# A hand-written instruction order for linear attention, Fourier mixing and a feed-forward block on one core

## The chip, the core and the metric

The kernel runs on one core of one Trainium2 chip. The metric is the device time of one execution in microseconds (us): the time of the core from start to end, median of the runs of a kernel. The program gives each of five engines its own list of instructions, and the traces show them side by side: PE (TensorE, matmuls; PEld is its weight load), DVE (VectorE), ACT (ScalarE), POOL (GpSimd) and SP (SyncE, which here only issues DMA). The program puts PE's results in PSUM tiles, from pools with two, one and three slots (`bufs` below), and its other tiles in SBUF. The profile shows the clock granted to PE as PEclk, where 1.00 is full speed and 0.50 is half.

## The reference, cut to what matters

```python
def phi(x):                                    # 64 -> 256 features
    proj = einsum('bhsd,df->bhsf', x, w_phi)
    proj = proj - max(abs(proj), axis=-1)
    return concatenate([exp(proj), exp(-proj)])
q_p, k_p = phi(q), phi(k)                      # batch 8, heads 8, tokens 576, head size 64
kv  = einsum('bhsf,bhsd->bhfd', k_p, v);  z = sum(k_p, axis=2)
x   = (q_p @ kv) / (q_p @ z + 1e-6)            # then heads side by side: 8 x 576 x 512

u   = x + real(fft(fft(x, axis=1), axis=2))    # Fourier mixing
un  = (u - mean(u)) / sqrt(var(u) + 1e-6)
out = u + maximum(un @ w_ch1, 0) @ w_ch2       # 512 -> 2048 -> 512
```

Everything is independent from batch to batch. One batch is four kinds of work: **features** (projections of keys and queries, their maxima, the exponentials), **heads** (kv and the quotient), **mixing** (the two Fourier transforms as matmuls with cosine and sine tables, then mean and variance), and the feed-forward block, **W1** and **W2**.

## The kernel before: the parts that matter

The order of the instructions is left to an automatic scheduler. The program text runs through a batch and tells the scheduler only that the end of W1 and W2 comes first:

```python
pj = tile_pool(name="pj", bufs=2, space=PSUM)   # projections, and pn_ of the heads
pk = tile_pool(name="pk", bufs=1, space=PSUM)   # kv
pb = tile_pool(name="pb", bufs=3, space=PSUM)   # psf (W1), pso (W2), pm, psD, px, pu (mixing)
...
for b in range(B):
    X = attention(b, loaded)              # features and heads
    if b + 1 < B:
        loaded = load(b + 1)
    mixed = mixing(b, X)
    if done is not None:
        ffn(b - 1, *done)                 # W1 and W2 of the batch before
    done = mixed
ffn(B - 1, *done)
```

A head is 10 matmuls into `kv`, a copy to `kvh` (ACT), 10 matmuls into `pn_`, then `tg`, `cb`, `rd` on DVE and the head's 64 columns of `X` on POOL. Mixing uses a symmetry: columns j and 512-j of X are added and subtracted ("folded") before the transforms.

```python
# mixing, before
pm = pb.tile([128, C]); matmul(pm, ones_f, X[0:1, 0, :])   # row 0 of X on all partitions
XC = X - pm                                                # DVE, ACT for the last half block
for sl in (slice(0, 2), slice(2, 4), slice(4, 5)):         # six folds
    for dst, op in ((CE, ALU.add), (CO, ALU.subtract)):
        nc.gpsimd.tensor_tensor(out=dst[:, sl, :], in0=XC[:, sl, 0:256],
                                in1=XC[:, sl, C:256:-1], op=op)
...                                                        # four small corner fixes on POOL
# psD, px, pu: the transforms on PE, casts on ACT, additions to X on DVE
def norm(c):
    ...                                                    # bn_stats, bn_aggr on DVE
    nc.gpsimd.tensor_scalar(out=UN[...], in0=X[...], scalar1=mean, op0=ALU.subtract)
    nc.sync.dma_start_transpose(out=UT[...], in_=UN[...])  # UT feeds W1
```

(These pieces are shortened; the whole text may follow.)

The softmax here doesn't subtract the row's maximum and nothing guards it: scores larger than these inputs give would overflow.

## Time and profile before

| | before |
|---|---|
| time, median of 2 runs | 818.63 us (817.53 to 819.73) |
| span of the profiled run | 812.1 us |
| mean granted clock of PE | 0.777 |
| one steady batch | 92.3 us |
| of it, W1 and W2 | 32.8 us |

The page of the profile, first part (busy us, share of the span, number of instructions), two rows of the span in 40 slices (PE's busy tenths, and PE's clock in tenths), and the chain of work that ended last:

```profile
span 812.1 us, 10263 instructions
PE 546.9 (67%) x3992; PEld 314.6 (39%) x3992; DVE 303.8 (37%) x612; ACT 312.1 (38%) x654; POOL 316.1 (39%) x381
...
PE   0005654669765895769765896749946797649995
...
PEclk9999995569855897559955797559955698559999
...
PE 47%; ACT 14%; DMA 12%; POOL 12%; DVE 11%; issue 2%; ACTq 0%; DVEq 0%; POOLq 0%
```

The reader should look at the rows PE and PEclk together: from the ninth slice on, seven times over, PE is denser at a clock of 8 or 9 (W1 and W2), and between these stretches half idle at a clock of 5. The chain passes through PE for less than half of the span. No engine is full, and the time is a sum of stages in which one engine after another is the limit.

DVE's timeline in the heads, two heads in a row (start, duration, engine, line, operation, and in brackets the idle time ahead of it and what ended it):

```profile
328.04 0.50 DVE L394 TENSOR_TENSOR tg<-pn__2803,E 128x325 f32<-128x325 f32 x1 [1.09 <-PE pn__2803 L387]
...
330.16 0.50 DVE L394 TENSOR_TENSOR tg<-pn__2834,E 128x325 f32<-128x325 f32 x1 [0.79 <-PE pn__2834 L387]
```

One head takes 2.12 us, and DVE waits in each for PE, whose matmuls run at half clock there (0.50 from 323.00 to 338.50). PE in turn waits 0.41 us in each head for the copy `kvh` on ACT.

### The profile page before, as it was taken

What the parts mean: (1) busy time and instruction counts of PE and PEld (TensorE: products, weight loads), DVE (VectorE), ACT (ScalarE), POOL (GpSimd) and SP (SyncE); (2) the same over time, 40 slices, a digit from 0 to 9 for tenths busy, and PEclk for the clock granted to TensorE, in tenths of its full rate; (3) what the DMA queues carried; (4) which work ended last, traced back from release to release, by engine and by line L of the source; (5) the groups of instructions that cost most, each with busy time, mean ns of one, the idle gap of its engine ahead of it and who ended that gap; (6) DMA issues with size and microseconds to landing.
All of it is one profiled execution on the core that took longest, in us unless ns stands there. A gap on an engine that the chain in (4) does not pass through costs nothing.

```text
span 812.1 us, 10263 instructions
## 1 busy us (share of the span) xinstructions
PE 546.9 (67%) x3992; PEld 314.6 (39%) x3992; DVE 303.8 (37%) x612; ACT 312.1 (38%) x654; POOL 316.1 (39%) x381
## 2 busy tenths in 40 slices
PE   0005654669765895769765896749946797649995
PEld 0003322426342552426342462516433363416472
DVE  5053535534335512535335412525136332414101
ACT  3094334336044524246044443246043452316060
POOL 7045584483037701384036800385004720243000
PEclk9999995569855897559955797559955698559999
DMA  8999347143242513233152512313120011001102
GB/s 94 181 122 140 33 63 99 14 53 56 62 57 36 80 31 70 27 56 56 54 63 37 72 37 55 40 29 56 39 50 2 7 37 45 2 0 30 43 19 57
DMA packets 115681, 42.66 MB, mean 53 GB/s; under 512 B 92080, under 2 KB 110512, under 8 KB 115632
## 3 DMA queue, kind: packets, MB, share of 16 engines
q0 software_dynamic: 52288, 18.40, 20.3%
q1 hardware_dynamic: 63344, 23.61, 14.6%
q8 instruction: 31, 0.51, 0.3%
q14 instruction: 18, 0.15, 0.1%
HBM read 36.77 MB, written 9.44 MB: 57 GB/s over the span
## 4 chain that ended last, share of the span: by engine, by line
PE 47%; ACT 14%; DMA 12%; POOL 12%; DVE 11%; issue 2%; ACTq 0%; DVEq 0%; POOLq 0%
PE psf L547 16%; PE pso L560 10%; DMA out_dram<-O 8%; DMA KT<-KS 4%; ACT QPHP L367 4%; DVE MQ L324 4%; ACT QPHN L367 4%; POOL CE L426 3%; POOL CO L426 3%; PE pu L486 3%; PE kv L378 3%; PE psD L451 2%; PE pm L411 2%; DVE cb L399 1%; DVE O L566 1%
## 5 line engine op out<-in xcount | busy, mean ns | idle before, releaser
L560 PE MATMUL pso<-W2b,HT 128*128 128x512 bf16 (+1 forms) x640 | 140.4, 379 | 0.0
L547 PE MATMUL psf<-UT,W1b 128*128 128x288 bf16 x1024 | 131.5, 286 | 6.8 <-ACT HT L553 5.0
L553 ACT ACTIVATE HT<-psf 128x288 bf16<-128x288 f32 x256 | 105.2, 411 | 67.1 <-PE psf L547 50.4
L547 PEld LDWEIGHTS <-W1b 128*128 128x128 bf16 x1024 | 99.3, 98 | 37.0 <-issue 10.9
L402 POOL TENSOR_TENSOR X<-cb,rd 128x320 f32<-128x320 f32 x64 | 46.3, 724 | 152.6 <-DVE rd L401 152.3
L566 DVE SCALAR_TENSOR_TENSOR O<-pso,rs,X 128x512 f32<-128x512 f32 (+1 forms) x40 | 30.0, 749 | 196.9 <-PE pso L560 156.3
L560 PEld LDWEIGHTS <-HT 128*128 128x128 bf16 (+1 forms) x640 | 63.6, 100 | 74.1 <-issue 3.4
L473 POOL TENSOR_SCALAR UN<-X,MV 128x512 bf16<-128x512 f32 (+1 forms) x40 | 61.9, 1559 | 9.2 <-DVE MV L472 8.9
L203 POOL DMA_DIRECT2D QS<-in_q_dram x8 | 7.5, 938 | 146.6 <-DMA QT<-QS 146.6
L275 PE MATMUL psk<-wphi,KT 64*128 64x128 bf16 x256 | 19.6, 303 | 61.8 <-ACT KPn L284 32.8
L383 ACT CAST kvh<-kv 128x130 bf16<-128x130 f32 x64 | 17.8, 278 | 103.3 <-PE kv L378 103.3
L451 PE MATMUL psD<-CS,CE 128*128 128x320 bf16 x80 | 28.5, 462 | 42.5 <-POOL CE L426 28.6
L387 PEld LDWEIGHTS <-QPHN 128*128 128x128 bf16 x320 | 34.6, 127 | 54.2 <-issue 54.2
L328 ACT ACTIVATE E<-MQ 128x16 f32<-128x16 f32 x8 | 1.8, 221 | 130.3 <-DVE MQ L324 130.3
L491 DVE TENSOR_TENSOR X<-pu,X 128x511 f32<-128x511 f32 x16 | 10.8, 673 | 104.5 <-PE pu L486 104.5
L279 DVE TENSOR_REDUCE MK<-psk 128x8 f32<-128x1024 f32 x32 | 38.1, 1206 | 17.6 <-PE psk L275 17.6
L293 POOL TENSOR_TENSOR VCn<-VS,VCn 128x512 bf16<-128x512 bf16 x32 | 33.9, 1059 | 27.0 <-ACT VCn L289 25.8
L275 PEld LDWEIGHTS <-KT 64*128 64x128 bf16 x256 | 11.9, 128 | 77.2 <-issue 46.3
L284 ACT ACTIVATE KPp<-psk 128x1024 bf16<-128x1024 f32 x32 | 32.9, 1029 | 21.5 <-DVE MK L279 21.3
L387 PEld LDWEIGHTS <-QPHP 128*128 128x128 bf16 x320 | 37.8, 133 | 3.5 <-issue 3.5
L324 DVE TENSOR_REDUCE MQ<-psq 128x8 f32<-128x1024 f32 x32 | 37.4, 1207 | 0.8 <-PE psq L317 0.8
L293 POOL TENSOR_TENSOR VCp<-VS,VCp 128x512 bf16<-128x512 bf16 x32 | 33.8, 1057 | 3.8 <-ACT VCp L289 3.8
(389 smaller groups left out, 928.2 us busy)
## 6 DMA issues: line engine op xcount, KB each, us to landing
KS<-in_k_dram POOLq DMA_DIRECT2D x8, 512.0 KB, 6.0
VS<-in_v_dram POOLq DMA_DIRECT2D x8, 512.0 KB, 6.2
out_dram<-O SPq DMA_DIRECT2D x32, 128.0 KB
out_dram<-O SPq DMA_DIRECT2D x16, 256.0 KB
QS<-in_q_dram POOLq DMA_DIRECT2D x16, 128.0 KB, 3.4
QS<-in_q_dram POOLq DMA_DIRECT2D x8, 256.0 KB, 4.9
W1b<-in_moe_w_ch_dram POOLq DMA_DIRECT2D x1, 2048.0 KB, 21.2
W2b<-in_moe_w_ch_dram POOLq DMA_DIRECT2D x1, 2048.0 KB, 33.8
```

The lines of the kernel that those rows point to most:

```text
L293: nc.gpsimd.tensor_tensor(out=VC[:, hs, :, 0:D], in0=VS[:, hs, :].rearrange("p h (j d) -> p h j d", d=D), in1=VC[:, hs, :, D:D + 1].to_bro ...
L324: nc.vector.tensor_reduce(out=mv_, in_=psq[:], axis=AX.X, op=ALU.max, apply_absolute_value=True)
L367: nc.scalar.activation(out=o, in_=psh[:], func=AT.Exp, scale=sgn)
L387: nc.tensor.matmul(pn_[:, i, 65 * c:65 * c + 65], lhsT=QP[:, h, 128 * c:128 * c + 128], rhs=kvh[:, i, :], start=True, stop=True,)
L402: nc.gpsimd.tensor_tensor(out=X[:, :, D * h:D * h + D], in0=cb[:, :, 0:D], in1=rd[:].to_broadcast([128, 5, D]), op=ALU.mult,)
L426: nc.gpsimd.tensor_tensor(out=dst[:, sl, :], in0=XC[:, sl, 0:256], in1=XC[:, sl, C:256:-1], op=op)
L451: nc.tensor.matmul(ps[:], lhsT=src[:, c, 128 * mt:128 * mt + 128], rhs=mat[:, c, :], start=(c == 0), stop=(c == 4),)
L473: nc.gpsimd.tensor_scalar(out=UN[0:M, c, :], in0=X[0:M, c, :], scalar1=mv[0:M, c, 0:1], scalar2=None, op0=ALU.subtract,)
L547: nc.tensor.matmul(ps[:], lhsT=W1b[:, cc, 128 * hh:128 * hh + 128], rhs=UT[:, cc, 288 * hf:288 * hf + 288], start=(cc == 0), stop=(cc == N ...
L553: nc.scalar.activation(out=HT[:, hh, 288 * hf:288 * hf + 288], in_=ps[:], func=AT.Relu)
L560: nc.tensor.matmul(po[0:M, :], lhsT=HT[:, hh, 128 * c:128 * c + M], rhs=W2b[:, hh, :], start=(hh == 0), stop=(hh == NHH - 1),)
L566: nc.vector.scalar_tensor_tensor(out=O[0:M, :], in0=po[0:M, :], scalar=rs[0:M, c:c + 1], in1=U[0:M, c, :], op0=ALU.mult, op1=ALU.add,)
```

## The change

The intent is to give PE one dense stream at full clock. The automatic scheduler goes, and the order is written by hand. Each kind of work becomes a generator that yields where it would have to wait, with the number of pieces of W1 or W2 to put there. There are two stages per batch: A weaves heads and mixing of batch b+1 into the 32 groups of W1 of batch b; B weaves the features of batch b+2 into the 40 pairs of W2 matmuls of batch b.

```diff
-    for b in range(B):
-        X = attention(b, loaded)
-        ...
-        if done is not None:
-            ffn(b - 1, *done)
+    def weave(lead, fill=None):        # run lead; after each "yield n", n pieces of fill
+        ...
+    def mixed_from(b, made):
+        X = yield from heads(b, made)
+        if b + 1 < B:
+            fetch(b + 1)
+        return (yield from mixing(b, *X))
+    with tc.manual_schedule():
+        ...                            # loads, constants, features(0), heads(0), mixing(0), features(1)
+        for b in range(B):
+            U, UT, mv = mixed
+            rs = scales(mv)
+            wide = widen(b, UT)                                        # W1, yields per group of 4
+            if b + 1 < B:
+                mixed, HT = weave(mixed_from(b + 1, made), wide)       # stage A
+            else:
+                _, HT = weave(alone(), wide)
+            slim = narrow(b, U, rs, HT)                                # W2, yields per 2 matmuls
+            made, _ = weave(features(b + 2, *ready[b + 2]) if b + 2 < B else alone(), slim)  # B
```

The order within the heads, with the folds now made per pair of heads and before the subtraction of `pm`:

```diff
-        for h in range(H):
+        order = (4, 0, 7, 1, 6, 2, 5, 3)
+        kvh = keyvalue(order[0])
+        yield 1
+        for i, h in enumerate(order):
+            nxt = keyvalue(order[i + 1]) if i + 1 < H else None
+            combine(h, kvh)
+            if i == 0:
+                nc.gpsimd.tensor_copy(out=X[:, :, C:C + 1], in_=X[:, :, 256:257])
+            elif h in (7, 6, 5):
+                fold(7 - h)            # two POOL ops: FEO = X +- X reversed, 64 columns
+            elif h == 3:
+                fold(3)
+            kvh = nxt
+            yield 1
```

And in mixing, with the subtraction after the fold (now on DVE) and UN moved from POOL to DVE:

```diff
+        yield 7
-        matmul(pm, ones_f, X[0:1, 0, :])        -> XC (DVE, ACT), six folds and four fixes (POOL)
+        matmul(pm, ones_f, FEO[0:1, 0, :, :])
+        CEO[64:128, 4] = pm[64:128]             # ACT
+        for i in range(2):
+            CEO[:, 0:4, i] = FEO[:, 0:4, i] - pm[:, i]     # DVE
+            ...                                 # two short ops for the last half block
+        yield 5
 ...
-            nc.gpsimd.tensor_scalar(
+            nc.vector.tensor_scalar(
                 out=UN[0:M, c, :], in0=X[0:M, c, 0:C], scalar1=mv[0:M, c, 0:1], ...
```

(Both are cut to their core; the lines without code syntax are summaries.) The matmuls of the reference's arithmetic are the same: PE has 3992 of them in both kernels.

## The prediction

> **What bounds the kernel now.** I read the page first: PE is busy 67% of 812.1 us, every other engine under 40%, so no engine is full. I then cut one steady batch (275.40 to 367.70 us, 92.30 us) into its six stages by the timeline of PE and asked for a table of windows:
>
> ```profile
> core 0: us, PE busy (x) PEld busy (x) DVE busy (x) ACT busy (x) POOL busy (x), PEclk, DMA share, GB/s
> 275.40:290.60 15.20, 15.04 (x121) 11.73 (x121) 8.01 (x22) 11.99 (x31) 7.42 (x5) 1.00 0.48 74
> 290.60:308.20 17.60, 17.60 (x88) 7.98 (x87) 3.00 (x4) 0.51 (x2) 0.00 (x0) 1.00 0.17 41
> 308.20:323.00 14.80, 4.85 (x46) 2.48 (x43) 4.14 (x4) 9.04 (x13) 2.40 (x4) 0.69 0.39 77
> 323.00:338.50 15.50, 12.57 (x150) 9.52 (x149) 8.03 (x21) 1.93 (x8) 6.34 (x9) 0.50 0.37 35
> 338.50:361.40 22.90, 11.73 (x69) 4.58 (x67) 9.07 (x10) 10.58 (x21) 17.40 (x24) 0.50 0.23 32
> 361.40:367.70 6.30, 5.77 (x37) 2.67 (x37) 3.86 (x11) 2.71 (x7) 5.01 (x6) 0.97 0.66 86
> ```
>
> The rows are W1; W2; the query maxima and exps; the eight heads; keys and folds; and the last matmuls of mixing. Only the first two (32.8 us) are dense at clock 1.00. The other 59.5 us wait on ACT, DVE and POOL in turn, mostly at clock 0.50, while W1 and W2 leave those engines partly or wholly free. The time of a batch is a sum of stages with different limits. The waits by line say the same: DVE and ACT idle through W2, POOL through the heads.
>
> ```profile
> DVE O L566 <- PE pso L560: 156.3, 31, 18.4
> POOL X L402 <- DVE rd L401: 152.3, 32, 43.3
> ACT E L328 <- DVE MQ L324: 130.3, 8, 20.8
> ...
> ACT kvh L383 <- PE kv L378: 103.3, 56, 1.9
> ```
>
> (columns: total wait, occurrences, longest). The chain of work alternates accordingly: W1 12.90, W2 10.37, then the output DMA 8.03, DVE 3.41, ACT, POOL CE/CO.
>
> [...] after a PE gap of 3.32 us before 312.00 the clock drops (0.65 in 313 to 316, then 0.50). [...] in the heads PE is recorded busy 12.57 of 15.50 us and stays at 0.50, so 65-column matmuls with pauses don't bring the clock back; the dense mixing matmuls do, at 361. [...]
>
> **The change, part by part** (durations are rows of the profile of before unless called an estimate).
>
> *Order.* Stage A of the loop weaves heads and mixing of b+1 into the 32 W1 groups of b; stage B weaves features of b+2 into the 40 pairs of W2 matmuls. PE then has, at full clock: W1 15.2; heads 160 matmuls, 54 ns apart at half clock, so 4.3 to 8.7, taken as 5.5 (estimate); pm 1.0 (half of 2.07); psD 20 x 0.134 = 2.7; px 0.7; pu 12 x 0.216 = 2.6: A = 28. B: W2 17.6 plus about 4 for projections (eight psq: 0.40 warm): 21.5. Floor of a batch: about 49 us against 92.3.
>
> *Removed.* XC (DVE 2.29 + 0.67), its copy, the six POOL folds and four corner fixes: the path from 346.27 to 359.10, 12.8 us per batch. UN leaves POOL (5 x 1.56 = 7.7).
>
> *Added.* Folds per pair: eight POOL ops over 128x320 f32, taken as X's 0.72 each: 5.8. CEO on DVE: two halves of XC (1.15 each) and two short ones of 0.67: 3.6. UN on DVE: 5 x 0.45 (the 128x512 f32 scalar op on gt took 0.41 to 0.48).
>
> *Engine sums per batch.* DVE: rs 3.5, heads 8 x 1.27 = 10.1, CEO 3.6, additions 3.6, five norms at 1.2 = 6; features 11.3, O 3.75: 42. ACT: relus 32 x 0.41 plus issue = 14, casts 5, features 18.6: 38. POOL: X and folds 11.8, load descriptors about 7.8, V scaling 9.7: 29. None exceeds PE's 49, so waits inside the weave decide.
>
> *Waits in A.* (1) Entry: the lead of B asks for 46 units but W2 has 40, so the last query piece comes after W2. ACT then has about 2.8 us left of exps, kvh of the first head is behind them in the FIFO, and the single kv buffer holds PE: 2.3, plus 0.8 to the first tg. (2) Heads: DVE sets the step, 1.27, against 2.12 before (323.92 to 326.04 and so on). PE needs about 1.1. The eighth head's rd is at 10.2 after the first tg. (3) POOL starts at 1.3, must do 16 operations of 0.72 with short waits: fold of the last pair ends at 13.2, two us after the seven W1 groups that should hide it. (4) pm 1.05, CEO first half 2.6 against 2.4 of W1, psD, px, one W1, casts: first pu ends at 22.0. (5) DVE tail: additions 1.45 + two norms 2.4, twice, then 0.65 + 1.2 = 9.6, to 31.6. pu and psf share three PSUM buffers; while pu1 and pu2 wait for DVE, psf has one or two, and steps in 1.14 us as in the trace of before (four matmuls per 1.14 to 1.15). The ten remaining W1 groups end at about 31. A = 3.1 + 31.5 = 34.6.
>
> *Waits in B.* psk holds its slot for DVE 1.21 then ACT 1.85 (in the trace ACT's exp follows the reduction), 3.6 with PE, and comes back after 3.2 of woven work: 4 x 0.45. B = 21.5 + 2 = 23.5. Batch: about 58 to 59.
>
> *Prologue.* Strict order puts the constants (DVE free of them at about 32: POOL's DMA issues until 11, its iotas until 15, then 17 us of DVE ops) ahead of features(0). Features alone: four pairs at 3.7 plus ACT 9.7 plus 1 = 25.5, to 57.5; heads(0) 14.5, to 72; mixing(0) half cold, DVE tail to 94; features(1) alone 25.5: first A at about 118.
>
> *Sum.* 118 + 6 x 59 + last A 34.6 + W2 17.5 + W1 15.2 + W2 17.6 + end 8.5 (O waits for a DMA, then the output, as in before) + 2 (O wait ahead of W1) = 567. The reported time exceeds the span by some 2 to 7 us (818.6 against 812.1): 570.
>
> **The rivals.**
> *R1, PE reaches its floor*: queues absorb my waits (POOL tail, entry). Batch 52, total 525. For it: cross-engine waits are short and each is written with filler behind it. Against it: the DVE chain in A alone is 3.5 + 10.1 + 3.6 + 9.6 = 27 and can't overlap itself.
> *R2, the clock stays low in A*: [...] Then a head step is 0.96 + 1.08 = 2.04 and W1 in A doubles until psD: about 12 more per batch, total 650. For it: the heads stayed at 0.50 before, and gap (1) follows the end of W2. Against it: the stall is under the 3.3 us that preceded the drop, and W1 groups fill half of each head step.
> *R3, FIFO blocking*: an O waiting for the output DMA (8.03 us for the 256 KB ones) or transposes of the next batch ahead of UT on SP hold back DVE or W1. O(4) comes two W2 rows of 4.4 us after O(2), so about 0.4 us; UT has all of B as slack. Worth 2 to 4 us a batch if I am wrong, total 590.
> *R4, scheduling gains nothing, since the old automatic order already overlaps*: the windows table refutes it; 59.5 us run outside W1 and W2.
>
> **Range and chances.** The batch period is the main uncertainty: 52 to 70 gives 525 to 635 with 6 periods; the prologue adds 10 either way. I centre on 570, with 528 to 635 for eight in ten, the upper side wider because R2 and R3 only add. To miss a 2% gain the batch would have to stay near 92; I give that 3% in all.
>
> **What would show each step.** PEclk near 1.00 through A and B, mean over 0.9 (R2: 0.5 to 0.7 in the heads). W1 starts near 118, not 183. Period of W1 starts 59: A 35, B 23.5. Head step about 1.27 by tg starts. pm waits for POOL's FEO about 2 us. psf waits for HT or DVE X late in A. PE gap of about 2.3 us at the entry of A behind ACT's exps. UN on DVE near 0.45, folds near 0.72: were POOL folds 1.2 or more, POOL would set the heads and A would grow by 4. The prediction would be wrong above all if the clock does not hold, or if the prologue's order costs far more than 118.

The sum came to 567 us for the span and 570 for the reported time. Statements about the hardware that rest on no run of this case are cut from the text, and the cuts are marked; no term of the sum is among them. Where the text says FIFO, the trace of before shows what is meant: `kvh` starts on ACT at 322.71, right behind the last of eight exponentials that follow one another from 315.46, though its `kv` matmuls had ended at 316.72; and DVE's `MQ`, whose matmuls had ended at 308.68, starts at 310.74, right behind an O that waited 4.73 us for the output DMA.

## The result, and the profile after

| | before | after |
|---|---|---|
| time, median | 818.63 us | 595.79 us (595.70 and 595.87) |
| span | 812.1 us | 594.1 us |
| granted clock | 0.777 | 0.951 |
| start of the first W1 group | 180.67 us | 114.31 us |
| one batch, start of W1 to start of W1 | 92.3 us | 63.7 us (mean of six) |

The ratio after to before is 0.7278, with a 95% interval of 0.7235 to 0.7320. A ratio is the mean time of one kernel's fast runs over that of the other's of the same rounds, so it isn't quite the ratio of the medians in the table. The output of every kernel in this document was correct.

The same parts of the page of the changed kernel:

```profile
span 594.1 us, 10224 instructions
PE 478.6 (81%) x3992; PEld 271.3 (46%) x3992; DVE 335.3 (56%) x668; ACT 304.7 (51%) x648; POOL 240.7 (41%) x325
...
PE   0125672598998899889988999988988998899894
...
PEclk9999995579998899999999899999988999999998
...
PE 36%; DVE 26%; POOL 16%; ACT 11%; issue 4%; DMA 4%; SPq 1%; POOLq 0%; DVEq 0%
```

PE is now dense from the ninth slice to the end. Its busy time even fell, by 68 us, for the same matmuls, because more of them ran at full clock (mean granted clock 0.951 instead of 0.777). But the clock is not 9 everywhere, and the chain still passes through DVE and POOL for 42% of the span: the woven stream still waits for those two.

The table of windows, for the one batch from 244.11 to 305.96 cut at four events (us, then busy us and number of instructions for each engine, granted clock, share of DMA, GB/s). The rows are: W1's first group to the first `tg`; the heads, to the start of `pm`; the rest of stage A; stage B.

```profile
core 0: us, PE busy (x) PEld busy (x) DVE busy (x) ACT busy (x) POOL busy (x), PEclk, DMA share, GB/s
244.11:247.57 3.46, 1.85 (x31) 1.33 (x30) 1.91 (x12) 2.79 (x6) 0.00 (x0) 1.00 0.25 81
247.57:262.95 15.38, 13.84 (x190) 10.20 (x188) 9.38 (x24) 7.78 (x21) 12.29 (x18) 1.00 0.01 4
262.95:280.75 17.80, 16.55 (x103) 9.56 (x103) 11.85 (x23) 8.86 (x21) 7.35 (x10) 1.00 1.34 155
280.75:305.96 25.21, 24.79 (x183) 10.56 (x183) 16.32 (x20) 17.46 (x33) 9.50 (x10) 1.00 0.33 68
```

PE is busy for 57.0 of the 61.85 us. In stage B it waits for 0.42 us altogether. The gaps are in A: 1.6 us at the entry, 1.5 us at `pm`, 1.25 us in the rest. PE's timeline shows each of them, and the make-up of a head:

```profile
246.37 0.19 PE L446 MATMUL kv<-V4p,K4p 64*128 64x65 bf16 x1 [1.60 <-ACT kvh L455]
...
248.84 0.65 PE L629 MATMUL psf<-UT,W1b 128*128 128x288 bf16 x4
249.43 0.20 PE L446 MATMUL kv<-V4p,K4p 64*128 64x65 bf16 x1
249.56 0.30 PE L450 MATMUL kv<-VCp,KPp 128*128 128x65 bf16 x4
249.79 0.20 PE L446 MATMUL kv<-V4n,K4n 64*128 64x65 bf16 x1
249.93 0.30 PE L450 MATMUL kv<-VCn,KPn 128*128 128x65 bf16 x4
250.07 0.19 PE L462 MATMUL pn__2833<-kvh,QPHP 128*128 128x65 bf16 x1
...
250.38 0.65 PE L629 MATMUL psf<-UT,W1b 128*128 128x288 bf16 x4
...
262.95 1.12 PE L502 MATMUL pm<-FEO,ones_f 1*128 1x512 f32 x2 [1.54 <-POOL FEO L436]
...
276.23 0.65 PE L629 MATMUL psf<-UT,W1b 128*128 128x288 bf16 x4 [0.50 <-ACT HT L634]
```

From one W1 group to the next, 248.84 to 250.38, is 1.54 us without a gap: 0.59 for the W1 group, 0.64 for ten `kv` matmuls and 0.31 for ten `pn` matmuls (31 ns each).

The `kv` matmuls aren't slower one by one. The last four, from 249.93 to 250.07, take 0.14 us, about as `pn` would; but the step out of each of the two matmuls whose weights have 64 rows (`64*128`), and the step into the second, take 0.13 us each. The starts of the single matmuls in this batch show the same at other changes of the weights' shape: 0.218 us from W1 to `kv` where W1 steps at 0.122, 0.311 from W2 to a projection where W2 steps at 0.216, and 0.310 from W2 with 128 weight columns to W2 with 64. PE changes the shape 68 times in this batch (51 times in a batch of the kernel before); at 0.095 us each that is, as an estimate, 6.5 of its 57.0 us.

At 262.95 PE has run out of W1 groups to put ahead of `pm` and waits for the last fold of POOL. POOL has been all but full since the X of the third head, as a window from there to `pm` shows (columns as above; POOL is the last of the five):

```profile
251.99:262.95 10.96, 9.42 (x121) 7.00 (x118) 5.81 (x15) 5.88 (x16) 10.64 (x15) 1.00 0.01 3
```

So although PE sets the step from head to head, 1.54 us, it is POOL's list that sets the start of `pm`. Later, at 276.23, W1 steps at 1.16 us instead of 0.50 per group, because two of the three PSUM slots of `pb` are held by `pu` until DVE has added them (the second from 276.30 to 277.65, the third from 280.24).

Last, a view of several periods shows that from the second on every other batch is slower, with the same work in it:

```profile
179.93:244.11 64.18, 59.59 (x503) 33.25 (x502) 39.45 (x78) 36.88 (x80) 29.12 (x37) 0.95 0.50 75
244.11:305.96 61.85, 57.03 (x503) 31.64 (x502) 39.46 (x78) 36.89 (x80) 29.14 (x37) 1.00 0.54 78
305.96:370.24 64.28, 59.69 (x503) 33.41 (x502) 39.46 (x78) 36.89 (x80) 29.15 (x37) 0.95 0.51 75
```

DVE, ACT and POOL do the same to 0.03 us; PE is busy 2.6 us longer at a mean clock of 0.95. Finer windows of the first of these batches find where:

```profile
184.20:187.30 3.10, 3.10 (x35) 2.16 (x35) 1.60 (x5) 0.70 (x3) 1.56 (x3) 0.50 0.00 0
187.30:190.30 3.00, 3.00 (x50) 2.15 (x48) 2.17 (x5) 1.36 (x4) 1.22 (x3) 1.00 0.02 5
```

After the gap at the entry, in which PE was busy for 0.40 of the 2.00 us from 180.50, the clock is 0.50 for some 3.4 us and then full again: 35 matmuls where the next stretch of the same length has 50. A second such patch lies behind the wait at `pm`. The other batches have the same gaps and no patch. (The first period, 65.62 us, is longer for another reason: it begins at clock 0.50, which the features of batch 1 alone had left, and stays there until 125.9.)

The trace shows something of what decides. The six patches begin at 183.9, 201.0, 310.2, 327.2, 436.5 and 453.5 (from windows of 0.25 us), so they are 17.0 to 17.1 or 109.2 us apart. With the length of a patch, 3.4 us, as the unit, these are 5 and 32 steps of 3.41 (109.2 / 32): the six fit one grid. Of the twelve gaps of 1.5 to 1.6 us at these two places in the six batches from 179.93 on, the six that fall whole or almost whole into one step of the grid are followed by a step at 0.50, and the six that a border of the grid splits are not; for the gap from 244.77 to 246.37 the border is at 245.3. It is a reading of one run and no rule: in run 8 a gap from 197.65 to 199.19 lies in one step of a grid laid through that run's patches (an estimate) and brings no patch; the 20 W1 matmuls behind it take 2.97 us, against 4.21 behind the gap before 261.95.

### The profile page after: what moved, and what is told of

Read it like the earlier page. It is cut to its first block, busy times and chain, and to the rows that moved or that the text cites. A ratio compares the mean times of both kernels' runs of the same rounds, so it can differ in the third digit from the quotient of the medians.

```text
span 594.1 us, 10224 instructions
## 1 busy us (share of the span) xinstructions
PE 478.6 (81%) x3992; PEld 271.3 (46%) x3992; DVE 335.3 (56%) x668; ACT 304.7 (51%) x648; POOL 240.7 (41%) x325
## 4 chain that ended last, share of the span: by engine, by line
PE 36%; DVE 26%; POOL 16%; ACT 11%; issue 4%; DMA 4%; SPq 1%; POOLq 0%; DVEq 0%
PE pso L645 13%; POOL FEO L436 8%; PE psf L629 7%; POOL X L477 6%; DVE MK L304 5%; DVE st L549 3%; PE psD L528 3%; ACT QPHN L388 3%; DMA out_dram<-O 3%; ACT QPHP L388 2%; DVE UN L551 2%; ACT KPp L309 2%; ACT KPn L309 2%; DVE MQ L341 2%; PE psk L300 2%
## 5 line engine op out<-in xcount | busy, mean ns | idle before, releaser
L629 PE MATMUL psf<-UT,W1b 128*128 128x288 bf16 x1024 | 156.2, 296 | 8.7 <-ACT HT L634 7.0
L645 PE MATMUL pso<-W2b,HT 128*128 128x512 bf16 (+1 forms) x640 | 154.1, 381 | 0.0
L645 PEld LDWEIGHTS <-HT 128*128 128x128 bf16 (+1 forms) x640 | 56.6, 100 | 66.8 <-issue 7.7
L436 POOL TENSOR_TENSOR FEO<-X 128x320 f32<-128x320 f32 x64 | 51.3, 823 | 2.5
L507 DVE TENSOR_TENSOR CEO<-FEO,pm 128x1024 bf16<-128x1024 f32 x16 | 19.5, 1221 | 45.0 <-ACT CEO L505 44.8
L300 PE MATMUL psk<-wphi,KT 64*128 64x128 bf16 x256 | 14.2, 235 | 34.1 <-DVE MQ L341 31.8
L388 ACT ACTIVATE QPHP<-psh 128x1024 bf16<-128x1024 f32 x32 | 33.0, 1031 | 12.7 <-PE psh L379 12.5
L388 ACT ACTIVATE QPHN<-psh 128x1024 bf16<-128x1024 f32 x32 | 33.0, 1031 | 0.0
L309 ACT ACTIVATE KPn<-psk 128x1024 bf16<-128x1024 f32 x32 | 32.6, 1018 | 0.0
L569 DVE TENSOR_TENSOR X<-pu,X 128x512 f32<-128x512 f32 x16 | 11.0, 688 | 34.8 <-PE pu L564 34.8
```

The lines of the kernel that those rows point to most:

```text
L300: nc.tensor.matmul(psk[:, jj, x, :], lhsT=KT[rr, 4 * pr + x, :], rhs=wphi2[rr, :], start=True, stop=True,)
L309: nc.scalar.activation(out=KP[:, hs, :, :].rearrange("p e (jp jj) f -> p jj (e jp) f", jj=2), in_=psk[:], func=AT.Exp, scale=sgn,)
L388: nc.scalar.activation(out=o, in_=psh[:], func=AT.Exp, scale=sgn)
L436: nc.gpsimd.tensor_tensor(out=FEO[:, :, i, a:a + D], in0=X[:, :, a:a + D], in1=X[:, :, C - a:C - a - D:-1], op=op,)
L629: nc.tensor.matmul(ps[:], lhsT=W1b[:, cc, 128 * hh:128 * hh + 128], rhs=UT[:, cc, 288 * hf:288 * hf + 288], start=(cc == 0), stop=(cc == N ...
L645: nc.tensor.matmul(po[0:M, :], lhsT=HT[:, hh, 128 * c:128 * c + M], rhs=W2b[:, hh, :], start=(hh == 0), stop=(hh == NHH - 1),)
```

## The experiments

Twelve kernels were run, all against the kernel before on the same chip. Two competing theories were tested first: **T1**, that the gain comes from weaving, because each stage fills the waits of the other and keeps the clock up; and **T2**, that it comes mostly from the cheaper arithmetic (folds and UN), and an order by hand is a detail. Then came the rest of the path: which of the waits seen above cost time. Runs with one execution are marked; their state is unknown, and they are read for differences of 5% and more.

### 1. No weaving at all (one run)

```diff
-                mixed, HT = weave(mixed_from(b + 1, made), wide)
+                mixed, _ = weave(mixed_from(b + 1, made))
+                _, HT = weave(alone(), wide)
...
-            made, _ = weave(features(b + 2, ...), slim)
+            made, _ = weave(features(b + 2, ...))
+            weave(alone(), slim)
```

> Both stages unwoven, arithmetic and all else as in the changed kernel. Theory (overlap): the two losses add up, 735 to 780 us, so that most of the 223 us gained comes from the weaving. Rival (new arithmetic): below 640 us.

Measured: 765.99 us, clock 0.803. The manual order with the new arithmetic, but one stage after another, keeps only 50 us (815.67 to 765.99 in the same session) of the 223. T2 would have kept most.

### 2. Stage A alone unwoven (one run)

Only the first half of the edit above.

> The changed kernel with heads and mixing of b+1 run alone, then the 32 W1 groups of b alone (only stage A unwoven). Theory (overlap): the chain of heads and mixing keeps its length of about 32 us and the 15 to 16.5 us of W1 are added behind it instead of lying inside: stage A about 48 us instead of 37, seven times, so 655 to 680 us. Clock at 0.5 in the heads. Rival (the new arithmetic is what counts, the order little): below 615 us.

Measured: 679.53 us, 83.7 more than the changed kernel, or 12.0 for each of the seven stages A. Its table of windows and DVE's timeline in the heads:

```profile
197.00:209.65 12.65, 6.97 (x95) 5.54 (x92) 7.00 (x18) 1.09 (x5) 11.39 (x16) 0.50 0.01 1
...
200.34 0.50 DVE L469 TENSOR_TENSOR tg<-pn__2009,E 128x325 f32<-128x325 f32 x1 [0.22 <-PE pn__2009 L462]
...
201.88 0.50 DVE L469 TENSOR_TENSOR tg<-pn__2042,E 128x325 f32<-128x325 f32 x1 [0.22 <-PE pn__2042 L462]
```

Without W1 between them the heads run at half clock, and a head takes 201.88 - 200.34 = 1.54 us: what it takes in the changed kernel *with* a W1 group inside. At full clock the 20 matmuls of a head take 0.95 us, at half clock 1.54, so in PE's list the W1 group rides in the time that the half clock wasted. The clock doesn't come back by itself: from 195.00 to 203.97 PE is recorded busy for 8.96 of 8.97 us and stays at 0.50, while in the changed kernel, with W1 between the heads, a patch ends after 3.4 us.

That is half of the mechanism. The other half is in the same row: PE is through with the heads at 203.97 and waits 5.68 us for POOL, which is as full here as in the changed kernel:

```profile
198.65:209.65 11.00, 5.32 (x73) 4.26 (x71) 5.82 (x15) 0.80 (x3) 10.67 (x15) 0.50 0.01 1
```

From the first `tg` to `pm` it is 15.36 us here (194.29 to 209.65) and 15.38 in the changed kernel: POOL's list sets it in both, and the fifteen W1 groups that the changed kernel puts there lie beside it.

### 3. Stage B alone unwoven (one run)

Only the second half of the edit.

> The changed kernel with features of b+2 alone, then W2 of b alone (only stage B unwoven). Theory (overlap): features alone take 25 us as in the prologue, W2 17.5 behind them, less 2.3 for the entry stall that W2 now hides: about 15 us more, six times: 670 to 700 us. Rival (new arithmetic): below 615 us.

Measured: 689.38 us, 93.6 more, or 15.6 for each of the six stages B that have features. Weaving A is thus worth 77 us while B is apart (765.99 - 689.38) and 84 when B is woven too (679.53 - 595.79); weaving B is worth 86 while A is apart (765.99 - 679.53) and 94 when A is woven too (689.38 - 595.79). The two stages gain almost independently.

### 4. The old automatic order with the new arithmetic (one run)

The kernel before, with the folds per pair, the order of the heads, `CEO` in place of `XC`, and UN on DVE; scheduler and program order as before.

> The kernel before, with its automatic order, and only the new arithmetic: folds per head pair in the new head order, subtraction after folding, UN on DVE. Theory (overlap): the path between pm and the last psD shrinks by 6 to 9 us per batch, eight times, so 745 to 775 us. Rival (new arithmetic is what counts): below 680 us.

Measured: 761.88 us, clock 0.804. The arithmetic alone gives 54 us of the 816 beside it, and the automatic order is no worse (761.88) than the manual order without weaving (765.99). So it isn't "by hand" that counts, but what stands beside what.

### 5. The new order with the old arithmetic (one run)

```diff
-        # FEO per pair in the heads, pm of FEO, CEO on DVE
+        # pm of X, XC on DVE and ACT, six folds and four fixes on POOL, as before
+        if 0 < b and b + 1 < B:
+            fetch(b + 1)           # the load issue moves behind POOL's folds
...
-            nc.vector.tensor_scalar(out=UN, ...)
+            nc.gpsimd.tensor_scalar(out=UN, ...)
```

> The changed kernel's order with the old arithmetic: pm, XC, POOL folds and corner fixes after all heads, UN on POOL; loads of the next batch issued behind the POOL folds. Theory (overlap): the path from the last X to the last psD grows by 7 to 9 us, of which W1 hides little, eight times: 645 to 675 us, so order alone brings about 155 us. Rival (new arithmetic is what counts): above 720 us.

Measured: 680.62 us, 6 above the expected range: a miss. Two lines of its waits (total us, times, longest):

```profile
POOL XC L506 <- DVE XC L503: 48.3, 8, 6.1
...
PE psD L539 <- POOL CE L511: 33.6, 16, 5.2
```

The chain `pm`, `XC`, fold, fix, `psD` stands in the woven order with too little W1 around it: PE idles for the folds, and the mean clock is 0.885 instead of 0.951. The estimate had counted the waits and forgotten the clock. What follows: order alone gives 137 us, arithmetic alone 54, both 223. The arithmetic is worth 85 us in the woven order (680.62 to 595.79), more than outside it; we read this as the weave needing short chains between engines, and no run tests that reading by itself.

### 6. All folds after the last head (one run)

```diff
-            elif h in (7, 6, 5):
-                fold(7 - h)
             elif h == 3:
-                fold(3)
+                for f in range(4):
+                    fold(f)
```

> The changed kernel with all eight fold operations after the last head instead of per pair. Theory (POOL's FEO is on the path to pm): 8 x 0.82 = 6.5 us after the last X instead of 1.6, so pm 4 to 5 us later in each batch, 625 to 645 us. Rival (PE order decides, folds are hidden by the seven W1 groups): under 605 us.

Measured: 635.88 us, 40.1 more (5.7 for each of seven stages A), clock 0.922. POOL's eight folds stand in one block of 6.28 us, and in the batch read PE waits for it at `pm` 4.94 us instead of 1.54. The same work, placed 3.4 us later than PE needs it, costs more than that wait. In the batch read (first `tg` at 259.60) the stretch behind `pm` is 2.56 us longer too, 20.36 instead of 17.80, and the clock is 0.50 in it for 6.8 us from 278.55 on.

### 7. UN back on POOL (3 rounds)

```diff
-            nc.vector.tensor_scalar(
+            nc.gpsimd.tensor_scalar(
                 out=UN[0:M, c, :], in0=X[0:M, c, 0:C], ...
```

> The changed kernel with UN back on POOL (1.56 us each there, 0.49 on DVE). Theory (the DVE tail of mixing holds the PSUM slots of psf and the first maxima of stage B): DVE loses 2.4 us per batch from its tail, POOL is idle there, UT is needed only 25 us later, so 1 to 2 us per batch gained, 582 to 592 us. Rival (moving UN to DVE was part of the gain): slower, 600 to 610 us.

Measured: 585.49 us median (582.91 to 588.11), ratio 0.7163 (0.7128 to 0.7198), against 0.7278 for the changed kernel. **One part of the change cost time.** The groups of UN in the kernel before and in the changed one (busy, mean ns; then the idle time before):

```profile
L473 POOL TENSOR_SCALAR UN<-X,MV 128x512 bf16<-128x512 f32 (+1 forms) x40 | 61.9, 1559 | 9.2 <-DVE MV L472 8.9
```

```profile
L551 DVE TENSOR_SCALAR UN<-X,MV 128x512 bf16<-128x512 f32 (+1 forms) x40 | 19.4, 485 | 1.5
```

DVE is three times as fast, and yet it is the wrong place. Nobody needs UN soon: it feeds W1 of the next stage A, a whole stage B later. But DVE's additions of `pu` wait behind it in DVE's list, and they hold the PSUM slots that W1 steps through. In the changed kernel the third addition starts 7.89 us after the first (272.35 to 280.24), with UN on POOL 5.73 us (266.62 to 272.35): 2.16 less, four UNs of 0.49 us that each held the list for 0.54.

Of the 10 us, 3.6 come at the start, where DVE's norms of batch 0 stand ahead of the features of batch 1 (the first W1 starts at 110.69 instead of 114.31). A batch without a patch gains 0.7 (61.15 against 61.85), 0.5 of it behind `pm`. The rest looks like clock: this profiled run had three patches where the changed kernel's had six, and of its four executions the two near 583 us have clocks of 0.959 and 0.962, the two near 588 us 0.954 and 0.953.

### 8. More W1 at the entry of A (3 rounds)

```diff
         kvh = keyvalue(order[0])
-        yield 1
+        yield 4
```

> The changed kernel with four W1 groups instead of one behind the first head's key-value product, so that PE has work during the stall of about 1.6 us at the entry of stage A. Theory: the first tg is set by the exps of ACT and comes no earlier, but the half-clock patch at the entry of every second batch (about 2.3 us) goes and three W1 groups fewer stand at the end: 1 to 2.5 us per batch, 580 to 590 us. Rival (stage A is a chain through POOL and DVE, PE's idle there is free and the patches too): 594 to 598 us.

Measured: 594.38 us (593.22 to 594.65), ratio 0.7267 (0.7244 to 0.7290): the same. The rival held. After the first stage A no half-clock patch is left at the entry (those behind `pm` stay), but what is filled there comes back elsewhere. In a batch without a patch (305.98 to 368.74) the first `tg` comes 4.37 us after the first W1 instead of 3.46, since the fourth W1 group itself waits 0.94 us for a PSUM slot; the rest of A takes 16.84 instead of 17.80; and stage B 26.17 instead of 25.21, because PE now waits for DVE at its second keys. In the batch before, with a patch, that wait is

```profile
285.30 0.40 PE L300 MATMUL psk<-wphi,KT 64*128 64x128 bf16 x8 [1.75 <-DVE MQ L341]
```

A gap of PE filled ahead of a chain that ends on DVE is only moved. Over the run, 3.1 us are gained ahead of the first `pm` and 2.5 lost in the six periods (table below).

### 9. The last folds on DVE (3 rounds)

```diff
+            eng = nc.vector if h >= 2 else nc.gpsimd       # in fold(h)
...
-            elif h in (7, 6, 5):
+            elif h in (7, 6):
                 fold(7 - h)
             elif h == 3:
+                fold(2)
                 fold(3)
```

> The changed kernel with the last two pairs' folds on DVE, issued after the last head's reciprocal, the first two pairs' on POOL. Theory (POOL's queue sets when pm starts): POOL ends with the last X about 1.6 us earlier, DVE, idle there, adds about 1.6 us in parallel or behind it, pm 0.5 to 2 us earlier in eight batches: 580 to 592 us. Rival (PE's head step sets it): 594 to 598 us.

Measured: 587.15 us (584.84 to 589.35), ratio 0.7176 (0.7144 to 0.7209). The wait at `pm` is gone. The four folds take DVE 2.19 us, 0.55 each, where POOL takes 0.82 and is behind with the X of the last heads.

### 10. The number tables ahead of the loads on POOL (3 rounds)

The constants need integer tables that POOL makes (iota) after it has issued the loads; in the changed kernel DVE's first operation on them waits 13.83 us for that.

```diff
-        clear_pads()
+        numbers = number()              # the iotas, split off generate_constants
         staged = load(0)
...
-        generate_constants()
+        clear_pads()
+        generate_constants(*numbers)
```

> The changed kernel with POOL's number patterns issued ahead of the loads instead of behind them. Theory (features of batch 0 wait for the constants on DVE, and these for POOL's patterns): DVE starts its constants about 9 us earlier, the first keys arrive 4 us later, 5 to 9 us gained: 587 to 591 us. Rival (the prologue waits for data): 594 to 600 us.

Measured: 587.41 us (584.54 to 588.01), ratio 0.7168 (0.7141 to 0.7195). The gain is a one-off at the start, as the table below shows.

### 11. The four together (four executions)

> The changed kernel with UN on POOL, four W1 groups at the entry of stage A, the last two pairs' folds on DVE, and the patterns first. Theory: the gains add (10 + 2 + 8 + 7 us), and the entry fill pays only now that the DVE tail is shorter: 562 to 576 us. Rival (each removes the same wait): 578 to 584 us.

Measured: **555.52 us** (554.85 to 556.02), ratio 0.6789 (0.6772 to 0.6807). This beats both kernels, and it is better than its expectation of 562 to 576, which is a miss too: 40.3 us under the changed kernel, where the four edits alone give 10.3 + 1.4 + 8.6 + 8.4 = 28.7. The page, and `pm` in PE's timeline:

```profile
PEclk9999995699999999999999999999999999999997
...
PE 61%; DVE 17%; ACT 12%; DMA 5%; issue 2%; SPq 2%; POOL 1%; DVEq 0%; POOLq 0%
...
239.78 1.09 PE L507 MATMUL pm<-FEO,ones_f 1*128 1x512 f32 x2
```

The chain is PE's for 61% instead of 36%, POOL is down to 1% of it, and once the first stage A has warmed up (at 106.9) no half-clock patch remains until the last output. Where the edits act is read from the starts of `pm` in the profiled run of each kernel (us; the first such `pm` belongs to the first stage A, the last to the seventh):

| kernel | start to first `pm` | six periods | last `pm` to end |
|---|---|---|---|
| changed kernel | 136.86 | 378.56 | 78.7 |
| UN on POOL | 131.39 | 371.51 | 78.2 |
| entry filled | 133.81 | 381.10 | 77.9 |
| last folds on DVE | 132.76 | 371.58 | 78.6 |
| tables first | 128.40 | 378.05 | 79.8 |
| all four | 122.17 | 354.57 | 76.4 |

In the six periods the single edits sum to -12.0 us, the four together give -24.0: the surplus is all there. A period of the combination lasts 58.95 us (221.48 to 280.43, clock 1.00), 2.9 under the patch-free batch of the changed kernel (61.85): six times that is 17 us, and the other 7 are the patches that are gone. Within the period, the first `tg` to `pm` takes 13.93 instead of 15.38, which is PE's own work there (13.84 busy) once POOL no longer ends it; the rest of A takes 15.62 instead of 17.80, stage B 25.03 instead of 25.21, and the entry 4.37 instead of 3.46. The entry fill, worth nothing where DVE then made PE wait, is worth something once UN is off DVE. That share was not separated by a run.

### 12. W1 behind every second head only (five executions)

With PE as the bound of a head's step (0.59 + 0.64 + 0.31), this version of the combination leaves out every second W1 group there.

```diff
             kvh = nxt
-            yield 1
+            yield i % 2
```

> The combined kernel with a W1 group behind only every second head (four fewer before pm, four more at the end of stage A). Theory (PE's own work sets the head step: 0.95 for 20 matmuls and 0.59 for a W1 group at full clock): the mean distance of the tg starts falls from 1.54 to between 1.25 and 1.35, where DVE's 1.27 takes over, and pm comes 2 us earlier, but what is saved there is mostly paid at the end of stage A: 544 to 557 us in all. Rival (POOL or the wait for the cast sets the step): tg starts stay 1.5 or more apart.

Measured: 563.97 us (563.61 to 567.86), ratio 0.6918 (0.6892 to 0.6945): slower than the combination, a miss in the total. DVE's timeline in the heads, and `pm` of the same batch in PE's:

```profile
230.68 0.46 DVE L473 TENSOR_TENSOR tg<-pn__2808,E 128x325 f32<-128x325 f32 x1
232.12 0.50 DVE L473 TENSOR_TENSOR tg<-pn__2845,E 128x325 f32<-128x325 f32 x1 [0.22 <-PE pn__2845 L466]
233.36 0.46 DVE L473 TENSOR_TENSOR tg<-pn__2878,E 128x325 f32<-128x325 f32 x1
...
242.74 1.09 PE L507 MATMUL pm<-FEO,ones_f 1*128 1x512 f32 x2 [0.70 <-DVE FEO L440]
```

After the first they are 1.44 to 1.50 and 1.24 by turns, 1.33 on average over the eight heads (229.51 to 238.83), so PE's own work did set the 1.54: that part of the expectation held. But from `pm` to the end of A now takes 17.60 us instead of 15.62, because the four groups run there at 0.50 each. From the first `tg` to `pm` it is only 0.70 less (13.23 against 13.93): PE's work there falls by 1.6 us (13.84 to 12.23), but PE idles for 1.0 us of the stretch instead of 0.1, and 0.70 of that is the wait for DVE's folds at `pm`. Work that is taken from one place of a full engine comes back in another, and DVE, at 1.24 a head, stands right behind PE.

## Why the prediction was right, and where it was off

The prediction of 570 us was 4% low, well inside its range. By its own steps:

- **The mechanism** (stages with different limits, put on top of one another; the clock follows, 0.803 unwoven and 0.951 woven) is shown by runs 1 to 5. R4, that scheduling gains nothing, is out by 137 us (run 5).
- **The ends of the program** were right: the first W1 at 114.31 us against 118, and 97.5 us from the last start of W1 to the end of the span against 95.4.
- **The period** carries the whole miss: 59 predicted, 63.7 measured (382.3 / 6), six times 4.7 or 28 us. Of the 4.7, 2.85 are in the patch-free batch (61.85). The other 1.86 are a mean over six: 7.2 us in all in the three batches with patches, 3.8 in the first, which starts at half clock, and 0.3 in the fifth.
- **The wrong term is PE's own work, "Floor of a batch: about 49 us".** PE is busy 57.0 us in the patch-free batch. The heads' 160 matmuls were taken as 5.5 us and need 8 x 0.95 = 7.6; a W1 group between them costs 0.59 and not 15.2 / 32 = 0.48; and stage B, put at 21.5 of work and 2 of waits, is 24.8 of work and 0.4 of waits. Most of it is one term that the sum lacked, the change of weight shape: 68 x 0.095 = 6.5 us as an estimate. The trace of before had it to see: in its heads a step is 0.054 us between `pn` matmuls, the figure that the prediction used for all 160, and 0.165 to 0.178 into and out of a 64-row weight. So the rival R1, "PE reaches its floor", was nearer the truth than it looked: the floor was not 49 but 57. The batch came out only 4.7 us long because the waits, put at 8.6 us, were 4.8: two errors that partly cancel, which is luck.
- **The head step** followed from it: "DVE sets the step, 1.27 ... PE needs about 1.1" is wrong; PE sets it, at 1.54. Run 12 shows it from the other side. (One of the two starts quoted for the old step is misread: the second `tg` starts at 325.92 and not 326.04. From there on the steps are 2.12.)
- **The start of `pm`** was put at 13.2 us after the first `tg` and came at 15.38. PE's own work accounts for 0.7 of the 2.2 (13.93 in run 11, where POOL no longer decides). The other 1.5 are POOL's list, which the prediction rightly had as the last to finish but took as 0.72 us per operation. X does take 0.723, but a fold takes 0.823 (its second operand is read backwards; no run separates that from the other differences of the two): the 14 operations from 251.99 to 262.84 start 0.775 apart, and they start later, since the third head's result is there at 4.4 us. That the wait at `pm` was 1.54 against the two predicted is partly luck: both of its ends were late.
- **The other stretches of A** were met nearly one by one: the entry 3.46 (3.1), from `pm` to the end 17.8 (18.3), W1 stepping at 1.16 (1.14) while `pu` holds the slots. Each was found in the trace before the kernel existed, by adding durations along the list of an engine.
- **R2, the low clock**, came in a small form. It was sized as all or nothing (12 us a batch); it is a patch of 3.4 us at two places in every second batch, 2.3 us in such a batch. The sum had no term for it.
- **R3, blocking by an output DMA**, is absent from the periods: DVE's wait of O for the output DMA, 4.7 us in each batch before, fell from 40.6 to 11.9 us in total, all of it behind the last stage A.
- **"UN leaves POOL"** was booked as work removed. Run 7 shows that its move to DVE cost 10 us in all. The prediction even listed the additions of `pu` behind the norms as the tail of A (9.6 us), and didn't ask whether UN had to stand in it.

What stays open: no run removes the changes of weight shape, so their cost is read from the steps alone. Nor do the runs show what sets PE's clock: of the twelve gaps of 1.5 to 1.6 us six brought a patch and six none, with their place on the grid, but run 8 breaks that reading.

## What to carry to other kernels

Weave stages that are bound by different engines, and count the densest engine's work from the steps between its instructions in a trace, with the changes of weight shape that the weave adds, since after the weave that sum comes near the time (57.0 of 61.85 us here). Then look which list ends last at each point where two engines meet: here POOL's did, though PE set the rhythm. Put an operation where the list of its engine is off the path, not where it is fastest (UN takes 0.485 us on DVE and 1.56 on POOL, and the kernel is 10 us faster with it on POOL), and look at what it holds while it runs (a PSUM slot, the next stage's maxima). After such a change single repairs give little and several together much: a gap that is filled only shows the next wait, until the chain is the bound engine's own.
